# Signs of the second weight's slices by ScalarE, and another order of all engines, in a gated-linear-attention and hardswish kernel

## The chip, the cores and the metric

The kernel runs on one core of a Trainium2 chip. Times are device microseconds (us) of one execution. The kernel before took 536.4 us, the median of three runs (536.31 to 536.47). The core's engines work side by side, each through its own queue in order: TensorE (PE, with its weight loads as PEld), VectorE (DVE), ScalarE (ACT), GpSimd (POOL), and SyncE (SP), which here only issues DMAs. They wait for one another by semaphores.

## What is computed

Attention (4 batches, 8 heads, 768 tokens, 48 channels a head) is a linear recurrence with a decay for each channel; its output, as a matrix of 3072 tokens by 384, goes through a feed-forward block with 2048 hidden units. In the reference, cut to what matters:

```python
for t in range(S):
    state = alpha[:, :, t, :, None] * state + np.einsum('bhd,bhe->bhde', k[:, :, t], v[:, :, t])
    y[:, :, t] = np.einsum('bhd,bhde->bhe', q[:, :, t], state)
x = y.transpose(0, 2, 1, 3).reshape(B * S, H * D)
h = x @ w_in                                  # 384 x 2048
g = h * np.clip(h + 3.0, 0.0, 6.0) / 6.0
out = g @ w_out                               # 2048 x 384
```

q, k, v and alpha are float32. w_in and w_out arrive as float64[...], so the kernel receives them as pairs of 32-bit words and makes float32 out of them.

## The kernel before

**Tiles.** The sequence is cut into 24 chunks j of 128 tokens, six to a batch; two chunks form a group g of 256 tokens, so there are 12 groups.

**Attention of a chunk.** `la`, `lk`, `lq`, `lv` load alpha, k, q, v. For j below 6 TensorE turns them (`ta`, `tk`, `tq`, four transposes each) and ScalarE copies alpha (`ca`); later chunks are turned on VectorE. `r` and `p` are two scans on VectorE that give the decays; `k` and `q` scale by them. `kb` and `ck` bring k into token order (from chunk 8 on by way of DRAM: `kt`, `kw`, `kr`). `sc` and `m` give the masked scores, `qa` and `sv` are ScalarE's copies that place q and the state beside them, `u` and `sm` update the state, `st` (GpSimd) decays it, `ya` and `yb` form the output on TensorE, and `cy` (ScalarE) keeps it as x.

**Feed-forward.** Groups 0 and 1 use plain matmuls for the first weight: `f.g.i` gives 256 of the hidden units, `fa` and `fb` the same for one chunk of group 0 at a time, so that work can begin when only chunk 0 is there. Each fills one of four PSUM banks, from which `fr` (ScalarE, L494) and `fg` (VectorE, L498) form g. Group 0 uses plain matmuls for the second weight too (`b`). From group 2 on the first product runs over combined operands: 25 sums of weight blocks (`y`), 11 sums of x in each group (`xc`), 20 products `M` of which each is four matmuls, kept (`n`), added up (`o`), gated (`e`, `h`). From group 1 on the second product is seven products `P` with sums `s` of g and four sums `x` of the weight; `K` and `G` take the results out of PSUM, `O` stores them.

**The weights' way to float32.** There are 16 slices: 0 to 7 of w_in (256 columns each, so that slice i is what `f.g.i` needs) and 8 to 15 of w_out (two of the 16 row blocks each). `w.i` loads a slice of 768 KB into one of five raw buffers, two of which lie in the space of g of group 1 and serve only slices 3 and 4; the slices of w_out go through three. On it work:

- `d1` (ScalarE, L186): the low word is scaled and rounded, in place.
- `d2` (ScalarE, L196): the magnitude of the high word is written as float32 to the weight's place.
- `d3` (VectorE): for slices in `BY_HALVES` two operations, a clamp (L203) and a shift (L205). For the others three: a clamp (L207), a shift with mask (L208) and an operation with two tensors that puts the sign and top bits back (L210).
- `dx` (ScalarE, L191), for slices in `BY_HALVES` only: writes a float16 zero with the sign of the number into the upper half of the low word, so that the sign comes with the low word.
- `d4` (GpSimd, L217): adds low and high words, as integers.

A raw buffer can be loaded anew when `d4` has read it.

**The order.** There is no scheduler at run time: `run()` near L750 splits one long string, and every word calls its step. The words' order is each engine's order, and the queue of DMAs on SP as well. `z.m.n` are n matmuls on the identity into bank m, which compute nothing that is used.

Of the kernel before, what the change touches and what calls it, by code (L numbers as in the profile page):

```python
# [17 lines left out]
def kernel(  # L18
# [42 lines left out]
    G = 2  # L61
# [114 lines left out]
    BY_HALVES = {0, 1, 2, 4}  # L176
# [395 lines left out]
    for i in range(8):  # L572
        r, o = divmod(i, 3)
# [176 lines left out]
    with tc.manual_schedule():  # L750
        run("""z.0.5 z.0.3 z.0.1 z.0.8 qa.0.0 w.0 d2.0 d3.0 la.0 ta.0.0 ca.0 r.0 lk.0 tk.0.1 k.0
               z.0.2 p.0 la.1 ta.1.2 lq.0 tq.0.3 ca.1 r.1 lk.1 lv.0.0 sv.0.0 d1.0 kb.0.0 ck.0 z.0.2
               u.0.2.1 sm.0.0 sv.0.1 q.0 qa.0.1 tk.1.0 k.1 p.1 z.0.2 sc.0.2.3 m.0 la.2 ta.2.0 ca.2
               dx.0 w.2 d2.2 kb.1.0 ck.1 lq.1 r.2 sm.0.1 st.1 tq.1.2 q.1 d3.2 z.0.3 d1.2 dx.2 lv.1.1
               u.1.3.1 sv.1.0 sm.1.0 p.2 sm.1.1 sc.1.0.2 m.1 ya.0.3 yb.0 cy.0 lq.2 w.1 d1.1 tq.2.1
               q.2 d4.2 lk.2 tk.2.3 k.2 fa.2.0 d4.0 st.2 sc.2.0.2 d2.1 d3.1 m.2 dx.1 d4.1 qa.1.1
               lk.3 la.3 ta.3.1 ca.3 la.4 fa.0.1 sv.1.1 w.3 r.3 ta.4.3 ca.4 r.4 tk.3.1 k.3 kb.2.0
               qa.1.0 d2.3 ya.1.2 yb.1 cy.1 fa.1.2 lq.3 ck.2 d1.3 p.3 d3.3 lv.2.2 u.2.3.2 sm.2.0
               d4.3 fb.2 tq.3.1 q.3 fb.1 qa.2.0 sm.2.1 sv.2.0 st.3 fr.0.2.0 fg.0.2 lk.4 tk.4.0
               sv.2.1 w.5 d2.5 k.4 d3.5 d1.5 qa.3.0 d4.5 qa.2.1 sc.3.1.3 m.3 w.6 d2.6 d1.6 d3.6 d4.6  # L760
               lv.3.0 lq.4 w.7 kb.3.2 fb.0 f.0.3.3 kb.4.0 ya.2.1 ck.3 u.3.3.2 sm.3.0 fr.0.3.1 fg.0.3
               fr.0.1.0 fg.0.1 qa.3.1 sv.3.0 sm.3.1 p.4 d2.7 sv.3.1 d1.7 d3.7 d4.7 f.0.5.0 fr.0.5.1
               fr.0.0.0 fg.0.5 fg.0.0 tq.4.3 ck.4 la.5 ta.5.2 f.0.6.3 ca.5 w.4 d2.4 ya.3.0 yb.3 cy.3
               fr.0.6.1 yb.2 cy.2 w.9 d2.9 q.4 qa.4.1 d1.4 d1.9 dx.4 la.6 w.8 d3.4 r.5 lk.5 w.10
               d3.9 p.5 ca.6 fg.0.6 d4.9 w.12 lq.5 lv.4.1 d2.8 d3.8 f.0.7.2 d1.8 st.4 d4.8 d4.4 w.11
               fr.0.7.0 fg.0.7 f.1.7.0 fr.1.7.1 fg.1.7 sc.4.0.2 m.4 f.1.1.1 fr.1.1.0 fg.1.1 f.1.3.3
               fr.1.3.1 d2.10 d1.10 tk.5.3 f.1.0.2 d2.12 d3.10 d4.10 w.13 fg.1.3 fr.1.0.0 fg.1.0 k.5
               d3.12 lq.6 f.1.6.0 f.1.2.1 u.4.1.0 sm.4.0 d1.12 d4.12 sv.4.0 qa.4.0 ya.4.2 fr.1.6.1
               fg.1.6 w.15 tq.5.3 fa.4.3 sv.4.1 d2.11 kb.5.1 d2.13 fr.1.2.0 f.1.4.2 fr.1.4.1 d1.11
               sm.4.1 q.5 r.6 d3.11 d3.13 fg.1.4 d4.11 lv.5.0 lk.6 tq.6 p.6 d2.15 d3.15 fg.1.2 d1.13  # L770
               d4.13 sc.5.0.3 yb.4 f.1.5.0 fr.1.5.1 fg.1.5 tk.6 m.5 b.1.0.2 fb.4 b.1.1 d1.15 d4.15
               st.5 y.5 w.14 la.7 lk.7 cy.4 d2.14 qa.5.1 ck.5 b.0.0.1 fr.0.4.0 d3.14 k.6 q.6 ca.7
               fg.0.4 d1.14 d4.14 x.0 y.1 y.10 b.0.1 y.0 y.2 u.5.2 P.1.0.0 K.1.0 qa.5.0 sv.5.0
               qa.6.1 P.1.1.3 b.0.2 b.1.2 kb.6.0 ya.5.3 y.6 s.1.0.0 sm.5.0 sv.5.1 G.1.0.0 tk.7
               s.1.1.1 s.1.2.3 x.1 yb.5 cy.5 b.1.3 sc.6.1.2 lv.6.2 ck.6 u.6.3.0 s.1.3.2 x.2 P.1.2
               b.0.3 K.1.1 y.7 s.1.4 s.1.5 y.11 y.3 r.7 xc.2.1 x.3 y.4 y.8 xc.2.3 k.7 xc.2.0 xc.2.4
               y.9 y.12 y.16 y.13 y.15 P.1.3.3 K.1.2 P.1.4 bo.1 P.1.5 xc.2.5 G.1.1.1 P.1.6 y.14 y.17
               y.19 xc.2.6 sm.6.0 G.1.2.2 y.20 M.2.0.2 lv.12.1 la.8 O.1.1 O.1.0 ca.8 y.18 y.21 y.23
               so.1 G.1.3.3 n.2.0.8 bo.0 lq.7 lv.7.0 O.1.2 m.6 xc.2.2 xc.2.10 xc.2.7 tq.7 r.8 p.7
               xc.2.8 sv.6.1 M.2.15.3 M.2.1 kb.7.3 n.2.1.9 M.2.16 M.2.2 n.2.2.10 M.2.7.0 n.2.7.11  # L780
               sm.6.1 xc.2.9 q.7 p.8 M.2.3 M.2.4 n.2.4.12 M.2.8 o.2.0.0 M.2.5 n.2.5.13 qa.7.0 sv.6.0
               st.7 lk.8 O.1.3 lq.8 lk.9 la.9 la.10 tk.8 tq.8 lq.10 lq.9 ya.6.1 yb.6 M.2.9 z.1.3
               M.2.18.1 o.2.1.0 e.2.1.1 M.2.10 cy.6 ck.7 sc.7.0.2 u.7.1.3 n.2.10.14 M.2.11 qa.7.1
               ca.9 la.11 y.22 M.2.6.2 h.2.1 q.8 m.7 e.2.0.0 h.2.0 n.2.11.15 qa.6.0 n.2.18.10 qa.8.1
               M.2.12 M.2.19 n.2.12.12 M.2.13 sm.7.0 sv.7.1 r.9 k.8 o.2.3.0 sv.7.0 ya.7.0 y.24
               o.2.5.0 n.2.13.12 o.2.2.0 yb.7 cy.7 sc.8.1.2 xc.3.1 o.2.2.1 e.2.2.1 xc.3.3 o.2.3.1
               M.2.14 xc.3.4 xc.3.0 xc.3.5 o.2.4.0 xc.3.7 xc.3.6 o.2.6.0 P.2.0.1 M.3.0.2 M.2.17
               h.2.2 o.2.6.1 e.2.3.0 h.2.3 o.2.7.0 K.2.0 n.3.0.12 M.3.1 n.3.1.9 e.2.5.1 M.3.7.0
               n.3.7.13 xc.3.8 o.2.7.1 xc.3.2 kt.8 e.2.6.0 h.2.6 tk.9 M.3.2 n.3.2.10 e.2.4.0 P.2.1.3
               h.2.4 h.2.5 s.2.0.14 e.2.7.0 G.2.0.1 h.2.7 M.3.3 M.3.4 n.3.4.8 k.9 s.2.1.11 M.3.8  # L790
               o.3.0.0 ca.10 kt.9 P.2.3.3 s.2.2.15 s.2.3.14 lv.8.2 kw.8 kr.8 lk.10 sm.7.1 xc.3.9
               M.3.5 n.3.5.11 K.2.2 e.3.0.1 xc.3.10 M.3.9 o.3.1.0 P.2.2 K.2.1 u.8.0.3 M.3.18.2 s.2.5
               M.3.10 n.3.10.14 n.3.18.15 e.3.1.0 s.2.4 P.2.4 tq.9 h.3.0 st.8 sv.8.0 M.3.11 n.3.11.8
               tk.10 p.9 sm.8.0 q.9 r.10 k.10 qa.9.0 qa.9.1 m.8 sm.8.1 h.3.1 M.3.19 o.3.5.0 kt.10
               P.2.5 G.2.2.0 st.9 M.3.12 sc.9.0.1 qa.8.0 n.3.12.10 o.3.3.0 kw.9 lv.9.0 kr.9 sv.8.1
               u.9.2.3 sm.9.0 sv.9.1 sv.9.0 G.2.1.2 sm.9.1 st.10 M.3.15.2 M.3.16 M.3.6.3 M.3.13 m.9
               o.3.4.0 o.3.6.0 tq.10 n.3.13.10 o.3.2.0 e.3.4.1 ya.8.2 yb.8 ya.9.3 yb.9 cy.9 M.3.14
               M.3.17 cy.8 xc.4.1 P.2.6 e.3.5.0 G.2.3.3 o.3.2.1 xc.4.3 h.3.4 xc.4.4 o.3.6.1 xc.4.5
               xc.4.0 xc.4.6 e.3.2.1 M.4.0.0 n.4.0.10 P.3.0.1 xc.4.7 o.3.7.0 p.10 h.3.5 o.3.3.1
               xc.4.8 M.4.7.3 M.4.1 xc.4.2 h.3.2 o.3.7.1 lk.11 O.2.2 tk.11 e.3.6.0 e.3.3.1 h.3.3  # L800
               P.3.1.2 e.3.7.1 n.4.1.13 M.4.2 K.3.0 ca.11 q.10 h.3.6 r.11 k.11 h.3.7 n.4.7.15
               lv.10.2 lv.11.0 kw.10 sc.10.0.1 kr.10 G.3.0.0 u.10.3.2 sm.10.0 qa.10.1 n.4.2.14 M.4.3
               M.4.4 M.4.8 s.3.0.9 xc.4.9 s.3.2.12 s.3.1.11 P.3.3.2 n.4.4.8 M.4.5 o.4.0.0 e.4.0.0
               sv.10.1 sm.10.1 xc.4.10 kt.11 O.2.0 O.2.3 lq.11 m.10 s.3.3.9 s.3.5 M.4.9 o.4.1.0
               P.3.2 sv.10.0 st.11 n.4.5.11 K.3.2 la.13 M.4.18.0 p.11 tq.11 lk.12 tk.12 K.3.1 M.4.10
               n.4.10.9 q.11 qa.10.0 n.4.18.12 e.4.1.1 la.12 s.3.4 ca.12 h.4.0 r.12 P.3.5 G.3.2.1
               h.4.1 M.4.11 P.3.4 n.4.11.8 M.4.12 n.4.12.14 qa.11.0 M.4.19 p.12 G.3.1.3 lq.12 kw.11
               O.2.1 tq.12 kr.11 u.11.3 sc.11.0.2 sv.11.0 O.3.1 lk.13 P.3.6 qa.11.1 M.4.6.2 G.3.3.2
               k.12 o.4.3.0 m.11 sm.11.0 sv.11.1 kt.12 M.4.13 n.4.13.14 q.12 o.4.3.1 e.4.3.0 o.4.2.0
# [123 lines left out]
```

## Time and profile before

| | |
|---|---|
| Median of three runs | 536.4 us |
| The profiled execution | 536.33 us |
| Its span in the profile | 534.5 us |
| TensorE: first matmul, first that counts, end of the last | 1.46, 7.46, 530.7 us |
| f.0.3 (first whole `f`) starts | 40.08 us |
| First product `P` starts | 94.13 us |
| First product `M` starts | 125.70 us |
| Sign operation on ScalarE, L191 | 4 times, 1.93 us |
| L203, L205 on VectorE | 4 times each, mean 0.86 and 0.70 us |
| L207, L208, L210 on VectorE | 12 times each, mean 0.71, 0.60 and 0.96 us |
| L217 on GpSimd, slices by halves and others | 4 times, mean 1.91 us; 12 times, mean 1.60 us (least 1.46) |

The span begins with the first instruction and ends with the last store's landing; some 1.8 us of the execution lie around it. A share of busy time is the union of an engine's instructions over the span. Matmuls overlap, so that the time from one start to the next (the pitch) is less than the duration of one, and the same holds, by less, for VectorE and ScalarE.

### The profile page before, as it was taken

The numbers are of one execution on the slowest core, as the hardware profiler recorded it, in microseconds if no ns is written. First come the engines' busy times: TensorE is split into PE (matmuls) and PEld (weight loads), VectorE is DVE, ScalarE is ACT, GpSimd is POOL, SyncE is SP. The second block draws the span as 40 slices with busy tenths as digits, with TensorE's granted clock in tenths as the row PEclk, the third lists the DMA queues.
The fourth block names the chain that finished last, engine by engine and source line by source line (L and its number), as shares of the span: only waits on it lengthen the run. The fifth ranks groups of instructions, "written<-read, shape, count | busy, mean of one in ns | idle before, by whom it ended". The sixth has DMA issues, their size and how long they took to land.

```text
span 534.5 us, 15145 instructions
## 1 busy us (share of the span) xinstructions
PE 524.2 (98%) x6306; PEld 498.9 (93%) x6306; DVE 477.1 (89%) x849; ACT 257.6 (48%) x503; POOL 50.4 (9%) x71
## 2 busy tenths in 40 slices
PE   7799999999999999999999999999999999999997
PEld 7698886789999999999999999999999999999996
DVE  6999989999999899998999999999999898586381
ACT  3889864212653553543644434642633544553330
POOL 5333435100000000000010000000000000000000
PEclk9999999999999999999999999999999999999999
DMA  9998877006615155254354455055364042100001
GB/s 174 215 255 256 208 220 164 7 2 158 149 32 121 28 132 130 50 136 101 82 109 113 95 124 139 20 129 122 81 144 97 18 97 48 36 3 1 29 1 44
DMA packets 124100, 54.40 MB, mean 102 GB/s; under 512 B 83328, under 2 KB 116864, under 8 KB 124032
## 3 DMA queue, kind: packets, MB, share of 16 engines
q1 hardware_dynamic: 124032, 53.44, 43.0%
q8 instruction: 49, 0.80, 0.7%
q14 instruction: 19, 0.16, 0.1%
HBM read 44.50 MB, written 8.91 MB: 100 GB/s over the span
## 4 chain that ended last, share of the span: by engine, by line
PE 88%; DVE 6%; POOL 2%; ACT 1%; DMA 1%; issue 0%; SPq 0%; DVEq 0%; POOLq 0%
PE m_ps L703 34%; PE m_ps L600 34%; PE m_ps L478 6%; PE t_ps L455 4%; PE t_ps L346 2%; PE t_ps L429 2%; PE m_ps L489 2%; DMA v<-in_v_dram 1%; PE m_ps L516 1%; DVE rings L647 1%; PE t_ps L282 1%; DVE raw L537 1%; ACT raw L191 1%; DVE g_sb L647 1%; DVE w L537 1%; POOL v L96 1%
## 5 line engine op out<-in xcount | busy, mean ns | idle before, releaser
L606 ACT COPY g_sb<-m_ps 128x512 f32<-128x512 f32 x110 | 63.7, 584 | 124.1 <-PE m_ps L600 101.3
L703 PE MATMUL m_ps<-w,g_sb 128*128 128x192 f32 x704 | 121.7, 327 | 0.0
L703 PEld LDWEIGHTS m_ps<-w,g_sb 128*128 128x128 f32 x704 | 113.7, 190 | 0.4
L703 PE MATMUL m_ps<-rings,g_sb 128*128 128x192 f32 x528 | 91.5, 326 | 0.0
L703 PEld LDWEIGHTS m_ps<-rings,g_sb 128*128 128x128 f32 x528 | 85.4, 190 | 0.1
L600 PE MATMUL m_ps<-xc,w 128*128 128x128 f32 x640 | 82.7, 277 | 0.3 <-DVE w L541 0.3
L600 PEld LDWEIGHTS m_ps<-xc,w 128*128 128x128 f32 x640 | 77.5, 192 | 1.5 <-issue 0.5
L494 ACT ACTIVATE r<-g_sb,half 128x512 f32<-128x512 f32 x80 | 57.0, 722 | 31.5 <-DVE g_sb L541 12.4
L498 DVE SCALAR_TENSOR_TENSOR g_sb<-r,g_sb 128x512 f32<-128x512 f32 x80 | 53.7, 682 | 6.8 <-ACT r L494 5.4
L600 PE MATMUL m_ps<-xT,raw 128*128 128x128 f32 x400 | 52.5, 277 | 0.0
L600 PEld LDWEIGHTS m_ps<-xT,raw 128*128 128x128 f32 x400 | 48.6, 192 | 0.6
L409 POOL TENSOR_TENSOR st<-sm,R 128x192 f32<-128x192 f32 x20 | 12.9, 643 | 353.7 <-DVE sm L439 295.7
L647 DVE TENSOR_TENSOR g_sb<-g_sb 128x512 f32<-128x512 f32 (+1 forms) x55 | 42.1, 793 | 1.3 <-PE m_ps L703 1.1
L600 PE MATMUL m_ps<-xT,w 128*128 128x128 f32 x320 | 42.0, 276 | 0.0
L600 PEld LDWEIGHTS m_ps<-xT,w 128*128 128x128 f32 x320 | 39.3, 192 | 0.1
L366 ACT COPY A<-q 48x256 f32<-48x256 f32 x88 | 35.5, 404 | 5.0 <-DVE q L332 3.7
L356 DVE TENSOR_TENSOR A<-t_ps,mask 64x256 f32<-64x256 f32 x96 | 36.0, 413 | 0.4
L478 PE MATMUL m_ps<-xT,w 128*128 128x256 f32 x144 | 32.8, 382 | 0.0
L600 PE MATMUL m_ps<-xc,raw 128*128 128x128 f32 x240 | 31.8, 276 | 0.0
L478 PEld LDWEIGHTS m_ps<-xT,w 128*128 128x128 f32 x144 | 26.7, 190 | 3.6
L309 DVE TENSOR_TENSOR_SCAN R<-t,ones 128x516 f32<-128x516 f32 x24 | 29.6, 1233 | 0.5 <-ACT t L300 0.4
L600 PEld LDWEIGHTS m_ps<-xc,raw 128*128 128x128 f32 x240 | 29.6, 192 | 0.1
(104 smaller groups left out, 730.3 us busy)
## 6 DMA issues: line engine op xcount, KB each, us to landing
raw<-in_moe_w_out_dram SPq DMA_DIRECT2D x8, 768.0 KB, 5.3
raw<-in_moe_w_in_dram SPq DMA_DIRECT2D x6, 768.0 KB, 7.1
v<-in_v_dram SPq DMA_DIRECT2D x48, 96.0 KB, 3.0
out_dram<-oh SPq DMA_DIRECT2D x44, 96.0 KB, 1.7
far<-kq SPq DMA_DIRECT2D x64, 64.0 KB, 2.2
kb<-far SPq DMA_DIRECT2D x64, 64.0 KB, 2.1
aq<-in_alpha_dram SPq DMA_DIRECT2D x36, 96.0 KB, 2.4
qq<-in_q_dram SPq DMA_DIRECT2D x36, 96.0 KB, 2.5
```

Source lines behind the costliest of these rows:

```text
L309: nc.vector.tensor_tensor_scan(out=reverse(R, n - 1, n), data0=reverse(ax, n, n), data1=reverse(ones, n, n), initial=0.0, op0=ALU.mult, op ...
L356: nc.vector.tensor_tensor(out=to[:, a], in0=sc[a][half], in1=mask[half, half].unsqueeze(1).to_broadcast([HB, NP, HB]), op=ALU.mult)
L366: nc.scalar.copy(out=to[:, a], in_=Q_t[j][64 * a : 64 * a + D, :, half])
L409: nc.gpsimd.tensor_tensor(out=st, in0=sm, in1=R_t[j][:, :, 0:1].to_broadcast([C, NP, D]), op=ALU.mult)
L455: nc.tensor.matmul(y_of(j, (i + 1) // 2, p)[:, HB * b : HB * b + HB], vb[:, p, e : e + 32], A_t[j][:, b, 2 * p + a], start=(b == 0 and i = ...
L478: nc.tensor.matmul(h[:, f], w1[:, kk, o : o + C], xT_t[g][:, kk], start=(kk == 0), stop=(kk == KT - 1))
L494: nc.scalar.activation(out=to, in_=h, func=AF.Relu, bias=half, scale=1.0 / 6.0)
L498: nc.vector.scalar_tensor_tensor(out=to, in0=r, scalar=1.0, in1=h, op0=ALU.min, op1=ALU.mult)
L600: nc.tensor.matmul(acc[g][i][:, f * C : (f + 1) * C], spots[w][:, f * C : (f + 1) * C], x_of(g, x), start=(first and f == 0), stop=last, s ...
L606: nc.scalar.copy(out=slots[z], in_=acc[g][i])
L647: nc.vector.tensor_tensor(out=out, in0=in0, in1=in1, op=ALU.subtract)
L703: nc.tensor.matmul(to[g], a, rhs[:, f], start=(first and f == 0), stop=(last and f == HF - 1), skip_group_check=True)
```

## The change

It has two parts. The first adds slices 8 to 15, all of w_out, to `BY_HALVES`: their `d2` gets another scale, their `d3` has two operations instead of three, each of them needs a `dx`, and `d4` reads the high word from the weight's place instead of the raw buffer. The second replaces the whole string of words: the same steps for everything else, with other banks and other places for kept tiles, in another order. The number of `z` matmuls is 29 in both. The eight `dx` are the only words added.

```diff
-    BY_HALVES = {0, 1, 2, 4}
+    BY_HALVES = {0, 1, 2, 4, *range(8, 16)}
...
-        run("""z.0.5 z.0.3 z.0.1 z.0.8 qa.0.0 w.0 d2.0 d3.0 la.0 ta.0.0 ca.0 r.0 lk.0 tk.0.1 k.0
-               z.0.2 p.0 la.1 ta.1.2 lq.0 tq.0.3 ca.1 r.1 lk.1 lv.0.0 sv.0.0 d1.0 kb.0.0 ck.0 z.0.2
-               u.0.2.1 sm.0.0 sv.0.1 q.0 qa.0.1 tk.1.0 k.1 p.1 z.0.2 sc.0.2.3 m.0 la.2 ta.2.0 ca.2
-               dx.0 w.2 d2.2 kb.1.0 ck.1 lq.1 r.2 sm.0.1 st.1 tq.1.2 q.1 d3.2 z.0.3 d1.2 dx.2 lv.1.1
...
-               s.11.1.14 s.11.3.10 P.11.3.2 K.11.0 s.11.2.11 o.11.2.1 o.11.3.1 P.11.2 K.11.2
-               e.11.2.0 h.11.2 s.11.4 e.11.3.1 h.11.3 P.11.1.0 s.11.5 G.11.0.1 O.11.0 O.10.3 K.11.1
-               P.11.4 G.11.1.2 P.11.5 G.11.2.1 O.11.2 P.11.6 G.11.3.0 O.11.3 O.9.2 O.11.1""")
+        run("""z.0.1 z.0.2 z.0.2 z.0.3 z.0.8 qa.0.0 w.0 d1.0 d2.0 d3.0 la.0 ta.0.0 ca.0 lk.0 z.0.3
+               tk.0.1 r.0 k.0 p.0 dx.0 d4.0 w.2 d2.2 d3.2 lq.0 lv.0.0 sv.0.0 z.0.5 z.0.2 kb.0.2
+               tq.0.3 q.0 ck.0 u.0.0.1 d1.2 dx.2 d4.2 sc.0.2.3 qa.0.1 sm.0.0 sm.0.1 m.0 la.1 ta.1.0
+               ca.1 r.1 p.1 st.1 ya.0.1 sv.0.1 yb.0 w.1 d2.1 d3.1 lq.1 tq.1.0 q.1 cy.0 fa.0.0 la.2
+               ta.2.2 d1.1 dx.1 lk.1 tk.1.3 k.1 fa.2.1 ca.2 r.2 kb.1.1 sc.1.0.2 m.1 qa.1.1 qa.1.0
+               lv.1.1 ck.1 u.1.3.1 sm.1.0 sv.1.0 d4.1 fa.1.2 w.3 d2.3 d3.3 sm.1.1 p.2 sv.1.1 ya.1.0
+               yb.1 lk.2 tk.2.2 k.2 st.2 d1.3 d4.3 lq.2 tq.2.3 q.2 cy.1 fb.0 fb.2 w.5 d2.5 fr.0.0.0
+               fg.0.0 d1.5 d3.5 d4.5 sc.2.0.1 m.2 qa.2.1 w.6 d2.6 qa.2.0 kb.2.2 fb.1 ck.2 w.7 d2.7
+               d3.7 f.0.3.3 fr.0.1.1 fg.0.1 d1.7 d4.7 la.3 ta.3.3 lv.2.2 sv.2.0 u.2.2.0 sm.2.0
+               f.0.5.0 fr.0.3.0 ya.2.1 d1.6 fg.0.3 d3.6 d4.6 sv.2.1 yb.2 f.0.7.2 fr.0.2.1 ca.3 la.4
+               w.4 lk.3 tk.3.2 d1.4 d2.4 dx.4 w.8 d2.8 d1.8 cy.2 dx.8 f.0.6.3 fg.0.2 sm.2.1 d3.4 r.3
+               k.3 d3.8 kb.3.3 lq.3 d4.4 tq.3.0 fa.4.1 lq.4 lv.3.0 ck.3 u.3.2.1 st.3 sv.3.0 p.3 q.3
+               qa.3.0 fr.0.6.0 sm.3.0 sv.3.1 sm.3.1 sc.3.0.3 m.3 fb.4 lk.4 tk.4.2 ta.4.1 w.9 fg.0.6
+               fr.0.5.1 fg.0.5 ya.3.0 qa.3.1 ca.4 yb.3 cy.3 d4.8 r.4 st.4 k.4 p.4 d1.9 fr.0.7.0
+               fg.0.7 fr.0.4.1 fg.0.4 la.5 lv.5.1 w.11 d2.9 d1.11 tq.4.3 q.4 ta.5.1 ca.5 f.1.3.3
+               kb.4.0 ck.4 fr.1.3.0 dx.9 f.1.7.0 fr.1.7.1 la.6 ca.6 d3.9 lv.4.2 u.4.2.1 r.5 sc.4.0.3
+               m.4 sm.4.0 d2.11 dx.11 sv.4.0 d4.9 d3.11 qa.4.0 w.10 d2.10 d1.10 dx.10 d4.11 fg.1.3
+               sm.4.1 st.5 lq.7 lk.6 tk.6 fg.1.7 d3.10 r.6 f.1.1.2 fr.1.1.0 f.1.0.1 lk.5 tk.5.0
+               fg.1.1 k.6 p.5 lq.6 w.12 d1.12 fr.1.0.1 k.5 fg.1.0 d2.12 d3.12 f.1.6.3 fr.1.6.0 dx.12
+               b.1.0.0 lq.5 tq.5.3 f.1.2.2 la.7 ca.7 fg.1.6 w.14 d1.14 lk.7 sv.4.1 fr.1.2.1 d2.14
+               lk.8 kb.5.2 qa.4.1 ck.5 dx.14 f.1.5.1 fr.1.5.0 d4.10 w.13 d2.13 d1.13 d4.12 w.15
+               d1.15 la.8 b.0.0.3 b.1.1 b.0.1 q.5 p.6 sc.5.0.1 d3.14 tq.6 fg.1.2 q.6 r.7 d3.13
+               s.1.1.1 d2.15 d3.15 dx.13 dx.15 fg.1.5 d4.14 y.0 y.1 u.5.3 ca.8 m.5 d4.13 lv.6.0 la.9
+               sv.6.0 f.1.4.2 sv.5.0 fr.1.4.1 fg.1.4 tk.7 d4.15 y.3 y.9 sm.5.0 b.1.2 b.1.3 P.1.0.1
+               P.1.1.2 kb.6.2 y.6 s.1.0.0 y.5 x.0 x.1 sv.5.1 ya.4.0 yb.4 qa.5.1 bo.1 qa.5.0 ya.5.1
...
+               h.11.2 o.11.3.1 e.11.3.0 h.11.3 P.11.1.2 G.11.0.0 O.11.0 K.11.1 P.11.4 K.11.2 s.11.5
+               G.11.1.0 O.11.1 P.11.5 G.11.2.0 O.8.3 O.10.3 P.11.6 G.11.3.1 O.11.2 O.9.1 O.11.3""")
```

## The prediction

> **What bounds the kernel now.** I read the busy shares first, then the chain of work that ended last, then the table of 10 us windows, and then the time lines of each engine up to 130 us and of the last 5 us. The page's shares and the windows:
>
> ```profile
> PE 524.2 (98%) x6306; PEld 498.9 (93%) x6306; DVE 477.1 (89%) x849; ACT 257.6 (48%) x503; POOL 50.4 (9%) x71
> ```
> ```profile
> 10.00:20.00 10.00, 6.87 (x104) 5.67 (x104) 9.31 (x17) 7.37 (x12) 0.09 (x1) 1.00 1.29 228
> 20.00:30.00 10.00, 8.84 (x208) 7.90 (x207) 9.84 (x19) 9.70 (x14) 6.81 (x5) 1.00 0.97 217
> ...
> 80.00:90.00 10.00, 10.00 (x44) 6.99 (x43) 9.83 (x14) 5.96 (x11) 5.97 (x10) 1.00 0.70 165
> ...
> 120.00:130.00 10.00, 9.71 (x71) 9.55 (x70) 9.87 (x23) 2.57 (x6) 0.00 (x0) 1.00 0.56 143
> ```
>
> The columns after the stretch and its length are PE, PEld, DVE, ACT, POOL, clock, DMA share and GB/s. TensorE is full in every window from 40 us on, but for 0.29 us at 127.9; VectorE is above 97% from 20 to 130 us in all windows but one (70 to 80: 85%). The chain's pieces say which of the two decides there:
>
> ```profile
> 108.89 2.34 DVE g_sb L647 x3
> 111.23 0.60 DVE raw L537
> ...
> 127.10 0.70 DVE w L541
> 127.80 0.14 issue
> 127.93 1.13 PE m_ps L600 x8
> ```
>
> From 92.1 to 127.8 the chain is VectorE almost without a break, and from 127.93 to 530.74 it is TensorE. So the first part is a balance of two full engines, which VectorE loses by 0.3 us, and the rest is pure matmul.
>
> To see where TensorE loses time I added up its work in the written order by pitch (starts, one after another, in the time line: a `P` product 2.60, an `M` product 0.90, a whole `f` 2.63, a half one 1.34, a `b` 2.60, four transposes 0.44, `sc` and `u` 0.62, `ya` or `yb` 0.59). Ahead of f.0.3 stand 26.7 us and it started at 40.08: 13.4 us lost. Ahead of M.2.0 stand 111.7, start 125.70: 14.0. Ahead of P.11.0 497.8, start 512.53: 14.7. **The loss is made before 40 us**; afterwards there is nothing to win but the tail. VectorE's sum before P.1.0 is 86.0 and P.1.0 began at 94.13, so VectorE had lost 8.1 us, all at the very start.
>
> **What the Trainium skill says.** "VectorE: DVE Perf Modes", section The perf-mode tier table: fp32 tensor_scalar runs at twice the rate of operations with two tensors. The trace agrees: L207 and L208 took 0.55 and 0.56 us for 768 columns, L210, which has two tensors, 0.96. "GPSIMD Engine Reference", section Key points: GpSimd shares its SBUF interfaces with VectorE and contends with two-port modes and two-input operations. The trace agrees: an L207 at 82.38, under a GpSimd add, took 1.77 instead of 0.56. "ScalarE: Activation LUTs", section What ACT_TABLE_LOAD costs: an operation with immediate scale takes 186 ns and 0.833 ns per element, 0.83 us for 768. The trace has 0.93 for the plain kinds (pitch 0.83), but 1.93 for the sign operation, which the page would not give; the measured value is used.
>
> **The change, part by part.**
>
> *VectorE.* For slices 8 to 15 the three operations L207, L208, L210 become two, L203 and L205:
>
> ```profile
> 52.17 0.68 DVE L203 TENSOR_SCALAR w<-w 128x768 f32<-128x768 f32 x1
> 52.89 0.69 DVE L205 TENSOR_SCALAR w<-w 128x768 uint32<-128x768 uint32 x1
> ...
> 69.04 0.55 DVE L207 TENSOR_SCALAR w<-w 128x768 f32<-128x768 f32 x1
> 69.62 0.56 DVE L208 TENSOR_SCALAR w<-w 128x768 uint32<-128x768 uint32 x1
> 70.22 0.96 DVE L210 SCALAR_TENSOR_TENSOR raw<-raw,w 128x768 uint32<-128x768 uint32 x1
> ```
>
> From start to start the pair took 1.33 and the triple 2.03 to 2.3 (mean 2.15). Eight times 0.82 is 6.6 us off VectorE, in its full stage.
>
> *ScalarE.* Eight sign operations, pitch 1.68 (16.72 to 18.39, 56.45 to 58.12): plus 13.4 us. Its sum from f.0.3 to f.1.4, the last `f` in the new order, is 51.3 us, while TensorE's over the same words is 53.7. In the old order the like stretch (f.0.3 to f.1.5) has 31.1 of 38.9. The cover has shrunk from 20% to 4%; the rival below is made of this.
>
> *GpSimd.* The low-half add takes 1.9 us instead of 1.5 (L217 by form: means of 1.93 and 1.86, against rows of 1.47 where nothing disturbs it): 8 times 0.4, 3.2 us, of a queue with 50 busy us in the whole span. It now waits for the sign operation too; behind it on GpSimd stand `st` and the next adds, behind those the state copies and `ya`. Its indirect cost is contention with VectorE: between 0 and the whole 3.2 us; I take 0.5.
>
> *The order.* The number of idle matmuls is 29 in both. I walked the new first 40 us by hand. Loads: the queue landed w.0 at 5.6, lq.0 (four small loads on) at 10.5 and lv.0 at 13.07 (two more), so a small load of 192 KB costs 1.2 us; slices two and three of the page (215 and 255 GB/s) then leave 2.6 us for a weight slice. In the new queue that gives w.2 10.6, lq.0 11.8, lv.0 13.0, la.1 14.2, w.1 16.8, lq.1 18.0, lk.1 20.4, w.3 24.2, lq.2 26.6, w.7 34.4, la.3 35.6, lv.2 36.8.
> VectorE, ends: d3.0 8.9, p.0 11.85, d3.2 13.2, q.0 13.8, m.0 15.95, p.1 18.3, d3.1 19.65, q.1 20.25, k.1 21.6 (0.75 waiting for lk.1), r.2 22.85, m.1 24.4, d3.3 27.4 (0.55 waiting for w.3), p.2 28.8, q.2 30.0, fg.0.0 30.6, d3.5 32.8, m.2 34.3, d3.7 37.5 (1.0 waiting for w.7), fg.0.1 38.1. Its work up to there is 28.0: lost 10.1, 2.0 more than before.
> ScalarE, next free: dx.0 10.3, dx.2 14.4, ca.1 15.8, d2.1 18.1 (waits for w.1, cy.0 behind it), cy.0 18.4, dx.1 20.9, ca.2 21.5, ck.1 23.6, d2.3 25.2, cy.1 27.3.
> TensorE: cy.1 is out at 27.3, then fb.0, fb.2, sc.2, kb.2, fb.1 bring f.0.3 to 32.8, with 22.8 us of work ahead of it: lost 10.0. Then ta.3 and u.2 wait 0.7 for their loads: 10.7, against 13.4. **TensorE gains 2.7 us.**
>
> That gain is worth what VectorE can follow. Behind the weights, the place where VectorE was nearest to TensorE in the old order is P.2.3, which needs s.2.1: TensorE's sum ahead of it is 146.3, VectorE's up to it 146.4. In the new order the nearest is P.2.2 with s.2.3: 149.6 and 145.2. The distance grows from -0.1 to 4.3, by 4.4 us (6.6 from the weights, the rest is spent by work placed earlier). Since there was nothing to spare at 127.9, VectorE allows 4.4 less its 2.0 more of early loss, less 0.5 of contention: 1.9. The smaller counts: **1.9 us**. Bounds: 0 (all of it eaten by loads that land late), and 3.7 (no early loss of 2.0 and no contention let VectorE allow 4.4, and no wait of 0.7 for ta.3 and u.2 lets TensorE gain 3.4, plus 0.3 from the wait at 127.9).
>
> *The tail.* In the kernel before, SP still issues three stores after the last output copy:
>
> ```profile
> 530.77 0.32 ACT oh L716
> ```
> ```profile
> 531.11 0.81 SPq L724 DMA_DIRECT2D out_dram<-oh  x2
> ```
> ```profile
> 531.97 0.43 SPq L724 DMA_DIRECT2D out_dram<-oh  x1
> ```
>
> Two of the three (O.9.2, O.11.1) had been ready for long. In the new order O.11.2 and O.9.1 stand ahead of O.11.3 and can go before 530.7, so only the first issue is left: 531.97 less 531.11 is **0.86 us**. From the start of the last issue to the span's end it stays 2.5. If SP is still behind, 0.4.
>
> *The M and P stage*, 130 to 530: the same products, TensorE full. VectorE's distance grows further from there in both orders (old 9.8, new 16.7 at the nearest places from sum 280 on); I cost the reordering at 0, from -0.3 to +2.
>
> Sum: 1.9 + 0.86 = 2.8. The profiled execution took 536.33 with a span of 534.5; 536.33 - 2.8 = 533.5. It stands 0.07 below the median, which I leave.
>
> **Rivals.**
> *ScalarE becomes the bound of the weight stage (slower).* It serves in order: `fr` empties the banks of `f`, and a sign operation, or a d1 or d2 whose slice has not landed, stands ahead of it. It decides once ScalarE waits over 3 us in all between 33 and 88 us (TensorE's 53.7 less 51.3, and some 0.6 for the last `fr`). For it: before, ScalarE waited 3.6 and 3.2 us for two single slices (L196). Against it: `fr` of f.1.4 has b.1.2, b.1.3 and P.1.0, 7.8 us, behind it on TensorE before its result is needed. With 8 us of waits TensorE is 5 late: 533.5 + 5 = 538.5. Chance 0.22.
> *Only the tail is won.* Three weight slices in the first seven loads hold back lv.0, la.1 and lk.1; if each small load costs 1.4 and each slice 3.1, w.7 lands 5 us later and the 1.9 is gone: 536.33 - 0.86 = 535.5, no change in the terms below. For it: the first 13 us ran at 174 GB/s only. Chance 0.16.
> *More is won than walked*, 3.7 and 0.86: 531.8, and up to 1 more if waits in the walk are all covered: 530.8. It is in the first case's upper end, with 0.04 beyond.
>
> **Numbers.** A measurement of this kernel can tell 0.2%, 1.07 us, from no change. Main case 0.58 (531.7 to 535.2), more 0.04: faster 0.62. Tail only: same 0.16. ScalarE: slower 0.22. The range goes from 530.8 to 538.5, with about half of the ScalarE case and little of the other end left out.
>
> **What would show it.** Right: P.1.0 and M.2.0 begin about 2 us earlier against their sums (M.2.0's 110.5 of work starting near 122.5), f.0.3 near 33, the last copy on ScalarE followed by a single store. VectorE without waits from 38 to 128. Wrong: TensorE gaps between 35 and 95 that end on ScalarE's L494 or L186 or on GpSimd's L217 (first rival), or f.0.3 after 35.5 with waits on loads (second).

## The result, and the profile after

The kernel after took 536.56 us (median of 20 runs, 535.12 to 539.16), the kernel before 536.57 in the same session (20 runs, 536.21 to 537.98): a ratio of 1.000, 95% interval 0.9993 to 1.0008. **No change, where 533.5 was predicted.** The profiled execution of after took 537.53 (span 535.8), 1.0 above its median, and that of before 536.33, 0.2 below; so the two traces differ by 1.2 us where the medians don't. Its executions also scatter over 4.0 us, twice those of before.

The page's shares after:

```profile
PE 523.3 (98%) x6306; PEld 499.6 (93%) x6306; DVE 476.1 (89%) x841; ACT 270.3 (50%) x511; POOL 55.7 (10%) x71
```

ScalarE has the 12.7 us more that eight sign operations were to cost (13.4). VectorE has eight instructions less, and yet only 1.0 us less, where 6.6 were predicted: **5.6 us of the saving don't show in VectorE's busy time.** Most of that are instructions that took longer, as the ledger below shows. The windows, in the columns of the prediction:

```profile
10.00:20.00 10.00, 7.15 (x152) 5.98 (x152) 9.53 (x15) 8.44 (x13) 4.73 (x4) 0.84 1.28 199
20.00:30.00 10.00, 9.54 (x189) 8.76 (x188) 9.79 (x17) 9.07 (x16) 1.85 (x1) 0.99 1.05 281
...
80.00:90.00 10.00, 10.00 (x37) 6.66 (x36) 9.27 (x10) 8.13 (x12) 3.68 (x2) 1.00 0.95 244
...
120.00:130.00 10.00, 8.64 (x112) 8.10 (x110) 9.93 (x20) 1.49 (x4) 0.00 (x0) 1.00 0.38 92
```

Between 80 and 90 us VectorE is 93% busy with 10 instructions, before 98% with 14. The chain of work that ended last, after:

```profile
81.85 8.53 DMA raw<-in_moe_w_out_dram
...
93.33 0.67 DVE g_sb L498
...
107.77 0.60 DVE raw L539
...
128.90 0.10 DVE q L332
...
129.74 0.61 DVE w L541
130.35 0.14 issue
130.49 2.52 PE m_ps L600 x20
```

From 93.33 VectorE leads the chain up to 130.35, 2.5 us longer than before. From 56.48 to there it runs mainly over three loads of the second weight (8.56, 6.85 and 8.53 us), other loads between them and one of GpSimd's adds, where before it was TensorE's up to 89.5; whether these loads decide is tested below. TensorE's waits up to 132 us (what waits, for what; total, times, longest) are now mostly for VectorE too:

```profile
PE t_ps L346 <- DVE q L332: 3.1, 2, 2.3
PE m_ps L600 <- DVE w L541: 1.6, 1, 1.6
PE t_ps L282 <- DMA rings<-in_q_dram: 1.5, 1, 1.5
```

By TensorE's sums, counted as in the prediction: 12.0 us are lost before f.0.3 (start 34.84; predicted 10.0, before 13.4), but 16.3 before M.2.0 (start 126.77; before 14.0). TensorE's early gain was lost again by 127 us. The tail is as predicted, one store behind the last copy:

```profile
532.97 0.32 ACT L716 COPY oh<-m_ps 128x192 f32<-128x192 f32 x1 [9.86 <-PE m_ps L703]
```

From the start of this copy to the span's end it took 2.79 us (532.97 to 535.76), before 3.75 (530.77 to 534.52): 0.96 won.

**Where VectorE's time went.** For each VectorE instruction up to the one at which M.2.0 begins, take its duration less the tenth percentile of the same line and shape in the same trace, and put it under "beside GpSimd" if a GpSimd instruction overlapped it. This ledger is good to about 1 us in its sums.

| us up to M.2.0 | idle | longer, beside GpSimd | longer, else |
|---|---|---|---|
| before | 7.5 | 4.4 | 0.5 |
| after | 10.2 | 9.1 | 1.1 |

In the kernel before, two VectorE instructions are over 0.5 us too long beside a GpSimd add (2.5 us together), in the kernel after seven (8.0 us). One of the seven, from VectorE's and GpSimd's time line:

```profile
87.09 1.86 POOL L217 TENSOR_TENSOR w<-w,raw 128x768 int32<-128x768 int32 x1 [5.27 <-ACT raw L191]
87.13 2.90 DVE L309 TENSOR_TENSOR_SCAN R<-t,ones 128x516 f32<-128x516 f32 x1
```

and the same pair 14 us before, the other way round:

```profile
73.02 1.23 DVE L309 TENSOR_TENSOR_SCAN R<-t,ones 128x516 f32<-128x516 f32 x1
73.34 2.56 POOL L217 TENSOR_TENSOR w<-w,raw 128x768 int32<-128x768 int32 x1 [1.84 <-DVE w L205]
```

The scan that began 0.04 us after the add ended 1.08 us after the add's end: it took almost its whole 1.22 us then. The scan that began first took its 1.23, and the add waited instead (2.56, not 1.86). So one holds the other up for whole instructions, and the first comer wins. This is what the Trainium skill says, "SBUF — State Buffer", section Who interferes with whom: VectorE shares a pair of SBUF ports with GpSimd, held for a whole instruction by whoever starts first; it is needed by VectorE instructions in a two-port mode or with two SBUF inputs, the latter only against a GpSimd instruction that reads SBUF. A scan has two inputs in SBUF. The prediction had cited only that there is contention, and priced it as if bandwidth were shared.

### The profile page after: what moved, and what is told of

Read it like the earlier page. It is cut to its first block, busy times and chain, and to the rows that moved or that the text cites. A ratio compares the mean times of both kernels' runs of the same rounds, so it can differ in the third digit from the quotient of the medians.

```text
span 535.8 us, 15118 instructions
## 1 busy us (share of the span) xinstructions
PE 523.3 (98%) x6306; PEld 499.6 (93%) x6306; DVE 476.1 (89%) x841; ACT 270.3 (50%) x511; POOL 55.7 (10%) x71
## 4 chain that ended last, share of the span: by engine, by line
PE 82%; DVE 9%; DMA 6%; issue 1%; SPq 1%; ACT 1%; POOL 0%; DVEq 0%; POOLq 0%; ACTq 0%
PE m_ps L600 34%; PE m_ps L703 34%; DMA raw<-in_moe_w_out_dram 4%; PE t_ps L455 4%; PE t_ps L346 2%; PE t_ps L429 2%; PE m_ps L478 2%; PE m_ps L489 2%; PE m_ps L532 1%; DVE raw L537 1%; DVE P L320 1%; DVE rings L647 1%; DMA kq<-in_k_dram 1%; PE t_ps L282 1%; DVE A L356 1%
## 5 line engine op out<-in xcount | busy, mean ns | idle before, releaser
L494 ACT ACTIVATE r<-g_sb,half 128x512 f32<-128x512 f32 x80 | 56.7, 722 | 48.4 <-DVE g_sb L541 24.9
L409 POOL TENSOR_TENSOR st<-sm,R 128x192 f32<-128x192 f32 x20 | 14.7, 736 | 344.9 <-DVE sm L439 287.4
L600 PEld LDWEIGHTS m_ps<-xT,w 128*128 128x128 f32 x320 | 39.2, 192 | 0.4
L309 DVE TENSOR_TENSOR_SCAN R<-t,ones 128x516 f32<-128x516 f32 x24 | 31.7, 1319 | 0.6 <-ACT t L300 0.5
L320 DVE TENSOR_TENSOR_SCAN P<-t 128x516 f32<-128x516 f32 x24 | 31.2, 1299 | 0.1
L537 DVE TENSOR_TENSOR g_sb<-g_sb 128x512 f32<-128x512 f32 x40 | 26.8, 683 | 4.7 <-ACT g_sb L606 4.5
```

What stands on the lines that cost most here:

```text
L309: nc.vector.tensor_tensor_scan(out=reverse(R, n - 1, n), data0=reverse(ax, n, n), data1=reverse(ones, n, n), initial=0.0, op0=ALU.mult, op ...
L320: nc.vector.tensor_tensor_scan(out=P_t[j], data0=aX[j % 2][:, 0:n], data1=ini[j % 2], initial=0.0, op0=ALU.mult, op1=ALU.add)
L494: nc.scalar.activation(out=to, in_=h, func=AF.Relu, bias=half, scale=1.0 / 6.0)
L537: eng.tensor_tensor(out=out, in0=in0, in1=in1, op=ALU.add if s1 > 0 else ALU.subtract)
L600: nc.tensor.matmul(acc[g][i][:, f * C : (f + 1) * C], spots[w][:, f * C : (f + 1) * C], x_of(g, x), start=(first and f == 0), stop=last, s ...
```

## The experiments

**Two theories.** Theory 1, contention: VectorE, which sets the start of M, lost what it had won by standing still beside GpSimd's adds. An instruction stands still when it has begun and doesn't advance; the trace shows it as a longer instruction, not as a wait. Theory 2: the new round of the weights' loads and buffers lets the weights land late, and TensorE waits for that.

### The parts alone

`order_only` has the new order without the new signs, `signs_only` the old order with them, `tail_only` the kernel before with two stores moved.

```diff
# order_only: after, with
-    BY_HALVES = {0, 1, 2, 4, *range(8, 16)}      and without dx.8 to dx.15
+    BY_HALVES = {0, 1, 2, 4}
# signs_only: before, with
+    BY_HALVES = {0, 1, 2, 4, *range(8, 16)}      and each dx.i ahead of d4.i
# tail_only: before, with
-    P.11.6 G.11.3.0 O.11.3 O.9.2 O.11.1
+    O.9.2 O.11.1 P.11.6 G.11.3.0 O.11.3
```

> The new order without the eight sign operations; slices 8 to 15 keep three VectorE operations, as before. Theory 1 (VectorE's 6.6 us went to contention with GpSimd's longer adds): VectorE gets the 6.6 us back as work but loses some 2 us of contention, M.2.0 some 3 to 4 us later than in the changed kernel, 539 to 541 us. Theory 2 (the weights' round of load, sign, add and buffer, behind it the queue of SP, makes TensorE wait between 50 and 96 us): each round is 1.7 us shorter on ScalarE and 0.4 on GpSimd, the waits of 1.5 and 0.7 us at 75 and 96 vanish, 536 to 538 us.

> The order of before, with the eight sign operations put in directly ahead of each slice's add. Theory 1: VectorE's gain of 6.6 us is worth 0.3 us here at most, since the order keeps TensorE full from 40 us on anyway; the longer adds cost little where the adds lie under operations with PSUM operands; 536.0 to 537.0. Theory 2: each slice's buffer comes free 2 us later, loads slip, TensorE waits for the last slices near 90 us: 537.5 to 540.

> The kernel before, with O.9.2 and O.11.1 put ahead of P.11.6, so that the last copy is followed by one store. Both theories: 0.86 us less, 535.5 to 535.8. If the last store's landing isn't what ends the run: no change.

| | median us (runs) | ratio to before, 95% interval |
|---|---|---|
| order_only | 544.23 (4) | 1.0136 (1.0120 to 1.0151) |
| signs_only | 539.72 (5) | 1.0057 (1.0044 to 1.0070) |
| tail_only | 535.46 (13) | 0.9979 (0.9971 to 0.9987) |

**The new order alone costs 7.7 us** (7.4 against the kernel before as it ran beside it), more than either theory had said, and the signs win 7.7 in it (6.7 in the profiled executions, 544.27 against 537.53). That this is near the 6.6 of the prediction is luck. The prediction took the pair's 1.33 us from a slice of w_in; for a slice of w_out after's time line has

```profile
66.02 0.55 DVE L203 TENSOR_SCALAR w<-w 128x768 f32<-128x768 f32 x1
66.61 0.56 DVE L205 TENSOR_SCALAR w<-w 128x768 uint32<-128x768 uint32 x1
67.08 0.68 DVE L498 SCALAR_TENSOR_TENSOR g_sb<-r,m_ps 128x512 f32<-128x512 f32 x1
```

that is 1.06 from the pair's start to the next instruction's, and 1.04 to 1.10 for all of slices 8 to 15 but one that stood still. The triple took 2.03 to 2.09 in order_only, where undisturbed. So some 8.0 us of work went (an estimate, eight times 1.0), and VectorE stood still 1.9 longer beside GpSimd than in order_only (9.1, not 7.2).

Most of the order's cost is in the ledger: 18.6 us up to M.2.0 (idle 10.9, beside GpSimd 7.2, else 0.5) against 12.4, so 6.2; the prediction's 2.2 of work placed earlier, less 0.96 of tail, make it 7.4, where the profiled executions differ by 7.9. Of the 6.2, 3.4 are idle time and 2.8 are beside GpSimd.

The signs alone, in the old order, cost 3.2 us, a time in theory 2's range. What VectorE waited for there fits the prediction's rival, in which ScalarE becomes the bound. VectorE's waits from 20 to 132 us in signs_only:

```profile
DVE g_sb L498 <- ACT r L494: 5.2, 5, 2.0
DVE w L203 <- ACT w L196: 2.9, 2, 2.2
```

It waited 3.9 us more for two of GpSimd's adds (L217). It sat idle for 17.7 us up to M.2.0, while ScalarE was 93% busy from 50 to 90 us; beside GpSimd it lost 4.2, no more than before. Neither the order nor the signs win without the other; only the tail does, with 1.1.

### The adds made small

`low_cut` and `cut_first` cover only a part of the columns in the adds named below, so that the weights lack most of their low parts. An add made small also ends sooner, and its raw buffer comes free sooner; the runs after these take that apart.

```diff
# low_cut: after, in add_low            # cut_first: the same for i == 0
+        if i >= 8:
+            dst, high, lo = dst[:, :, 0:16], high[:, :, 0:16], lo[:, :, 0:16]
```

> The changed kernel, whose adds for slices 8 to 15 cover 32 of the 768 columns, so that 96 per cent of the second weight is left without its low part; all waits stay. Theory 1: the stalls of VectorE under these adds (0.8, 1.7 and 1.7 us between 74 and 95) are gone, M.2.0 starts 3 to 4 us earlier, 532.5 to 534. Theory 2: the round is 1.8 us shorter, the waits at 75 and 96 us shrink by that, but VectorE is not earlier than by 1 us: 535 to 536.

> The changed kernel, with the add of slice 0 alone cut to 48 of its 768 columns, so that most of this slice lacks its low part. Theory 1: the scan L320 that took 2.89 us under this add takes 1.2, f.0.3 starts 1.2 to 1.7 us earlier than 34.84, the end is 1 to 1.7 us earlier, 535 to 535.5, since VectorE is the bound at M.2.1. Theory 2: f.0.3 is earlier, the end is not: 536.2 to 537.

`low_cut` took **533.47** (4 runs; ratio 0.9942, 0.9923 to 0.9961), 3.1 less than after: the time predicted for the change. VectorE's busy time, in low_cut's page, fell by 4.5 us though it has the same work:

```profile
PE 523.6 (98%) x6306; PEld 500.0 (94%) x6306; DVE 471.6 (88%) x841; ACT 270.7 (51%) x511; POOL 42.9 (8%) x71
```

`cut_first`, with one add small, took 535.37 (20 runs; 0.9979, 0.9971 to 0.9987), also as theory 1 had it; its profiled execution, 538.3, was the slowest of its 20, so that its trace doesn't show the median's gain. The add of slice 0 stands beside the first scan of p:

```profile
10.65 1.85 POOL L217 TENSOR_TENSOR w<-w,raw 128x768 int32<-128x768 int32 x1 [3.65 <-ACT raw L191]
10.70 2.89 DVE L320 TENSOR_TENSOR_SCAN P<-t 128x516 f32<-128x516 f32 x1
...
15.55 0.69 PE L346 MATMUL t_ps<-q,k 48*64 48x64 f32 x32 [2.28 <-DVE q L332]
```

That is after's time line. The scan came 1.67 us late, q.0 behind it, and TensorE waited 2.28 us for q.0.

### The loads

```diff
# queue: after, with lq.5 ahead of w.12
# short_load: after, in load_weight for slices 8 to 15
-                out=to, in_=moe_w_out[o : o + m * C, :]
+                out=to[:, :, 0:192], in_=moe_w_out[o : o + m * C, 0:192]
```

> The changed kernel with lq.5 put ahead of w.12 in SP's queue. Its wait of 1.47 us on TensorE at 75 us goes in any case. Theory 1: VectorE is late at M.2.1 all the same, 536 to 536.7. Theory 2: 1 to 1.5 us less, 535 to 535.6.

> The changed kernel whose loads of slices 8 to 15 bring only the first quarter of each row; the rest of the raw buffer holds what was there, so that most of the second weight is wrong. All waits stay, the loads land 3 us earlier or more. Theory 1: 535.5 to 536.5, only VectorE's waits of some 2.5 us between 60 and 100 us shrink. Theory 2: 533 to 534.5.

They took 537.12 (12 runs; 1.0006, 0.9994 to 1.0019) and 537.02 (12 runs; 1.0008, 0.9999 to 1.0016). Both are about 0.5 us above what theory 1 had expected, and 2 to 3 above theory 2. Neither a quarter of the bytes nor another place in the queue helps, though in short_load no load of the weights stands in the chain any more (it runs mainly over ScalarE up to 67 us and over VectorE from 70 us), and in queue TensorE's wait of 1.5 for q is gone. **Theory 2 alone falls.** That both bounds lie close together, so that shorter rounds would pay once VectorE stands still less, isn't excluded by these runs.

### The adds cut in pieces

The whole add is done, in several instructions.

```diff
# split_add: after, all slices; split_some: slice 0 by 256, 8 to 15 by 192, others whole;
# split_two: as split_some, but 8 to 15 by 384
-        nc.gpsimd.tensor_tensor(out=dst..., in0=high..., in1=lo..., op=ALU.add)
+        for m in range(dst.shape[1]):
+            for n in range(0, dst.shape[2], cut):
+                at = slice(n, n + cut)
+                nc.gpsimd.tensor_tensor(out=dst[:, m, at]..., in0=high[:, m, at]..., ...)
```

> The changed kernel with every low-half add on GpSimd cut into pieces of at most 256 and 192 columns (three for a slice of the first weight, four for one of the second), nothing left out. Theory 1 (VectorE operations with two SBUF inputs or in a two-port mode stand still until a GpSimd add that has begun is over, and the adds of 1.85 us cost VectorE 9.1 us up to 132 us, 4.4 before): the stall per meeting is at most a piece, the sum falls to 4 to 6 us, 532.5 to 534.5. Theory 2 (the round of the weights' loads decides): the round isn't shorter, 536 to 537.

> The kernel after, with only the adds that ran into VectorE's work cut in pieces: slices 8 to 15 in four pieces of 192 columns, slice 0 in its three rows of 256; the others whole. In the run with all adds cut, slice 4 was late by the cutting and TensorE waited 1.43 us for it. Contention theory (VectorE stands still while a whole GpSimd add runs): VectorE's stretch under adds falls from 9.1 to 3.5 to 4.5 us, no wait for slice 4, 534.0 to 535.5. If what the pieces cost on GpSimd is what limits them: like the run with all adds cut, 535.8, or later.

> As the run before this one, but slices 8 to 15 in only two pieces of 384 columns. Contention theory: if VectorE waits at most for the end of the piece that runs, it waits about half as long as for a whole add; stretch 5 to 7 us, 535 to 536.3. If what counts is the sum of the time in which adds run, whatever their pieces: 536.6, as after.

(In split_add the w_in slices came out in six pieces, 192 and 64 columns in each of three rows, not three.)

| | median us (runs) | ratio to before, 95% interval | beside GpSimd |
|---|---|---|---|
| split_add | 535.78 (21) | 0.9985 (0.9978 to 0.9991) | 3.9 |
| split_some | 536.27 (14) | 0.9996 (0.9981 to 1.0010) | 5.5 |
| split_two | 535.80 (21) | 0.9986 (0.9978 to 0.9994) | 7.2 |

**Inconclusive in size.** VectorE's loss beside GpSimd fell in all three traces, but the medians fell by 0.3 to 0.8 only, less than theory 1 expected but for split_two; split_some is not distinct from before. The profiled executions of split_some and split_two took 534.37 and 535.05, below their medians, so those traces show a good case. So of low_cut's 3.1 us it is not shown how much came from less standstill and how much from the rounds, which it shortened too; pieces with short loads, or the kernel before with small adds, were not run. In split_add the cutting had a price of its own, a later slice 4 (TensorE's time line):

```profile
49.39 1.16 PE L493 MATMUL m_ps<-xT,w 128*128 128x128 f32 x8 [1.43 <-POOL w L220]
```

### The adds doubled, and a control

Fewer or shorter adds also leave GpSimd free and release buffers earlier. `double_add` does each add of slices 8 to 15 a second time into dead space, `busy_memset` two memsets of that space, about as long, in its place.

```diff
# double_add: after, behind the add, for i >= 8
+            nc.gpsimd.tensor_tensor(out=hi.bitcast(I32), in0=dst.bitcast(I32),
+                                    in1=lo.bitcast(I32), op=ALU.add)
# busy_memset: in its place
+            for _ in range(2):
+                nc.gpsimd.memset(hi.bitcast(FP), 0.0)
```

> The kernel after, and GpSimd does a second add of the same size behind each add of slices 8 to 15 (two inputs in SBUF, result into the spent high word of the raw buffer, which nothing reads). The weight itself is ready as early as before; the raw buffer comes free some 1.9 us later and GpSimd has 15 us more to do. Contention theory: VectorE's stretch under adds grows from 9.1 us by as much again as slices 8 to 15 cause, 4 to 6 us, and the time to 539 to 542. If what counts is only when buffers come free and when GpSimd is done (occupation theory): it and the next run come out alike.

> The control to the run before it: behind each add of slices 8 to 15 GpSimd does two memsets of the spent high word instead of a second add, so that it is occupied, and the buffer held, for about as long, but reads nothing from SBUF. Contention theory: stretch clearly less than with the second add, and 536.5 to 538.5. Occupation theory: the same time as with the second add.

`double_add` took **547.62** (5 runs; ratio 1.0209, 1.0191 to 1.0227), `busy_memset` **539.59** (5 runs; 1.0054, 1.0042 to 1.0067): 8.0 us apart. The same scan of chunk 6, in double_add beside the second add (L220; line numbers are three higher here):

```profile
87.95 1.85 POOL L220 TENSOR_TENSOR raw<-w,raw 128x768 int32<-128x768 int32 x1
88.08 2.81 DVE L323 TENSOR_TENSOR_SCAN P<-t 128x516 f32<-128x516 f32 x1
```

and in busy_memset beside the memsets (L221):

```profile
85.20 1.68 POOL L221 MEMSET raw<- 128x768 f32 x2
85.46 1.23 DVE L323 TENSOR_TENSOR_SCAN P<-t 128x516 f32<-128x516 f32 x1
```

By the ledger VectorE lost 16.9 us beside GpSimd in double_add and 9.0 in busy_memset, against 9.1 in after: the second adds cost 7.9, the memsets nothing in the sum, and 7.9 is close to the difference of the two times. The scan was held up by the GpSimd instruction **that reads SBUF** and not by the one that only writes, as the skill's page says of VectorE instructions with two SBUF inputs. The clamp and the shift, each with one SBUF input, were held up by memsets too, also in busy_memset:

```profile
66.64 1.97 POOL L221 MEMSET raw<- 128x768 f32 x2
66.92 0.95 DVE L203 TENSOR_SCALAR w<-w 128x768 f32<-128x768 f32 x1
67.90 1.13 DVE L205 TENSOR_SCALAR w<-w 128x768 uint32<-128x768 uint32 x1
```

instead of 0.55 and 0.56. That fits the page's other case, the two-port modes, which contend whether GpSimd reads or not; the trace doesn't show the mode. Occupation costs something else: busy_memset is 3.0 us later than after, 1.1 above what theory 1 had expected of it and far below double_add. VectorE was idle 2.7 us longer (12.9, not 10.2): a constant memset of kq (L257) stood behind more work in GpSimd's queue, and VectorE waited 4.0 us for it (2.4 in after), and 1.1 for the last of the new memsets themselves. double_add waits for kq as well (4.3 us) and came out 5.6 later than theory 1's expectation.

### The new order with small adds

`order_low` is order_only with low_cut's edit.

> The new order without the eight sign operations (544.2), with the adds of slices 8 to 15 covering only 32 of their 768 columns, so that the output is not the reference's. Contention theory: that order too has 7.2 us of stretch under adds, of which these eight adds cause 3 to 4; so 540.3 to 541.5. If the cut adds helped the kernel after by having the weights ready earlier, and not by contention: 543.5 to 544.5, because here they wait for VectorE's third operation in any case.

540.92 (5 runs; ratio 1.0075, 1.0062 to 1.0088), as the contention theory had it: 3.3 less than order_only, and the ledger beside GpSimd fell from 7.2 to 5.2. Small adds win about the same with and without the signs on ScalarE, and signs_only, with the signs in the old order, lost no more beside GpSimd than before: **it is the order that put the adds in VectorE's way**, not the wait for the sign. In that order the signs then added 1.9.

### TensorE's clock early on

```diff
# warm: after, with
+    z.0.8 z.0.8 ahead of sc.0.2.3
```

> The kernel after, with 16 more idle matmuls ahead of the first scores, where TensorE waited 2.28 us and then ran at a granted clock of 0.84 for some microseconds (64 small matmuls took 2.01 us, not 1.10). If that loss of clock counts, TensorE wins up to 1.4 us before the first f; but VectorE is the engine that sets the start of M, so the contention theory expects 536.0 to 536.8, no difference. If TensorE's early loss is what takes the gain: 535.0 to 535.6.

538.83 (7 runs; ratio 1.0036, 1.0021 to 1.0051), outside both expectations, by a mistake of mine: the 16 matmuls took 3.84 us, not the 1.8 assumed, and pushed the scores 1.6 us back (17.13, after 15.55). The clock stayed at 1.00 as meant, but f.0.3 began 2.1 us later. So the loss of clock isn't priced by this run; what it shows is that 1.6 us of delay at 15 us come out as 2.3 at the end. There is no slack.

### The old order with pieces, and a better version

`tail_split` is tail_only with split_some's edit. `early_memset3` is after with the constant memsets of L257 done at the load of v of chunk 1; `early_two3` is that and split_two's edit.

```diff
# early_memset3: after, in load_akq
-        if j < FIRST + NQ:
-            for o in (BLK, 3 * BLK):
-                nc.gpsimd.memset(to[o : o + BLK, :, V - 1, D - BLK : BLK], 1.0)
# in load_v
+        if j == 1:
+            for to in quads.values():
+                for o in (BLK, 3 * BLK):
+                    nc.gpsimd.memset(to[o : o + BLK, :, V - 1, D - BLK : BLK], 1.0)
```

> The kernel before with the two ready stores moved ahead (535.46) and with the adds of slices 8 to 15 in four pieces of 192 columns, slice 0 in three. In the old order VectorE lost 4.4 us under adds, 2.6 of them between 80 and 100 us, and VectorE sets the start of M there. Contention theory: stretch about 2.5 us, so 533.5 to 534.8. If the adds' pieces end later than whole ones and TensorE then waits for the weights: 535.5 or later.

> The kernel after, with GpSimd's constant memsets of the turning buffers (L257) done all at once with the load of v of chunk 1, not with the first loads into each buffer, where they stand in GpSimd's queue behind the adds: VectorE waited 2.37 us for one at 70.41. Contention theory, with VectorE as the engine that sets the start of M: 534.2 to 535.5, the stretch under adds unchanged at about 9. If that wait is covered (TensorE being the bound there): 536.2 to 536.8.

> As the run before it, and the adds of slices 8 to 15 in two pieces of 384 columns, slice 0 in three (535.80 alone). Contention theory: both gains add up, 533.4 to 534.8, ahead of both kernels. If the pieces' gain was chance: as the run before it.

`tail_split`: 535.16 (14 runs; 0.9976, 0.9968 to 0.9984), not distinct from tail_only and above the 533.5 to 534.8 that theory 1 had expected. VectorE lost 1.4 us less beside GpSimd (3.1, not 4.5), but in the old order TensorE is as full as VectorE, and P.1.0 began at 94.90, in tail_only at 94.83. `early_memset3`: 536.37 (14 runs; 1.0000, 0.9992 to 1.0008), no gain, where theory 1 had expected 1.1 to 2.4. The wait for kq is gone, but the next in line took its place: VectorE's waits from 60 to 132 us,

```profile
DVE w L203 <- ACT w L196: 1.5, 1, 1.5
DVE g_sb L499 <- ACT r L495: 0.5, 1, 0.5
```

`early_two3`: **534.48** (6 runs; 0.9963, 0.9949 to 0.9976), ahead of both kernels by 2.1, and of split_two by 1.3. Why the early memsets win with pieces and not without is not settled; the traces show a like idle time (8.9 and 9.7) and a like loss beside GpSimd (7.3 and 7.4).

## Why the prediction was wrong

- **VectorE's 6.6 us**: under-sized. The pair was read off a slice of w_in (1.33); on the slices that changed it took 1.06, so some 8.0 us of work went. With the order held fixed the profiled executions differ by 6.7 only because more standstill took the rest.
- **ScalarE's 13.4 and the rival made of it**: 12.7 in busy time. No wait of TensorE in after ends on L494 or L186, and VectorE's waits for ScalarE between 60 and 132 us sum to 1.0. One wait of TensorE, 0.7 us at 96 us, ends on L217. The rival (538.5) didn't happen here; in the old order it did.
- **Early loss of VectorE, 2.0 more**: 2.7 more idle, a little under-sized, and not where it was put: up to 40 us after is only 0.2 above before (5.3 and 5.1). The largest single wait after 40 us, 2.4, is at 70 us, for the memset of kq behind the adds in GpSimd's queue.
- **TensorE's 2.7**: it lost 1.4 less before f.0.3, as the scan beside the first add delayed q.0.
- **GpSimd's contention, 0.5, with 3.2 as its bound: this is the step that failed.** It measured 4.7 (9.1 less 4.4). The bound was wrong in kind, though the prediction's own example, an L207 of 1.77 instead of 0.56, had stood still for 1.2. It took the part by which the adds grew longer, 8 times 0.4, as all that could collide. But a collision costs up to the whole add (1.67 us for a scan beside an add of 1.86), and whether it happens is set by what the order puts beside the add. In the order before, most adds lay beside VectorE instructions with an operand in PSUM, which ran at their usual time, as this one from before's time line:

```profile
67.24 1.28 DVE L498 SCALAR_TENSOR_TENSOR g_sb<-r,m_ps 128x512 f32<-128x512 f32 x2
67.46 1.47 POOL L217 TENSOR_TENSOR w<-raw 128x768 int32<-128x768 int32 x1 [2.14 <-ACT r L494]
```

  In the new order more lie beside scans, multiplications and the weights' clamps, whose inputs are in SBUF. I had costed the contention of the edit and not that of the order. By the ledger 2.8 of the 4.7 came with the order alone and 1.9 with the signs in it.
- **The allowance of 1.9**: 4.4 of distance less 2.7 less 4.7 less 0.6 of other lengthening is -3.6, not +1.9. TensorE's further loss at M.2.0 in the two profiled traces is 2.3. With 8.0 in place of 6.6 the distance is 5.8 and the sum -2.2; the ledger's error of 1 us allows no closer test.
- **The tail's 0.86**: 0.96 by the traces; alone it won 1.1.
- **M and P stage, 0**: right. From M.2.0's start to the last matmul's end it took 405.0 before and 406.2 after, and M.2.0 stands 1.2 us of work earlier in the new order.

So the medians' sum is a tail of 1.1 won and a weight stage of about 1.1 lost. low_cut, which has fewer collisions (4.3 us by the ledger), took 533.47, the predicted time. That is in part luck: its rounds are shorter too, and the prediction had VectorE's saving too small and TensorE's early gain too large.

## What to carry to other kernels

Before an order is changed, list for every long GpSimd instruction what VectorE does beside it; put such instructions beside VectorE work that ran at its usual time here (with a PSUM operand, or transposes), and price a collision at up to the whole length of the first comer, not at a share. Take a duration from the very tiles that change. Compare an engine's busy time with its instruction count: work was taken away here and the busy time stayed, which shows stalls inside instructions that no list of waits contains. Where two engines are full together, a gain in the one is worth only what the other can follow, so look for the next wait before counting it.

## What the runs showed of the hardware

- A VectorE instruction in its way stands still for the rest of a GpSimd add: scans of 1.22 us took up to 2.90, a clamp L203 of 0.55 up to 2.20 (in double_add), a multiplication from SBUF of 0.66 took 1.49. Adds beside instructions with a PSUM operand cost VectorE nothing, nor did an add beside a transpose, which kept its 1.13 (at 79.75 in after). Beside memsets of GpSimd scans kept their 1.22, while a clamp took 0.95 and a shift 1.13.
- The order of start decides, and a lead of 0.04 us was enough: a scan was late by 1.68 us in one case and the add by 0.70 in the other. Whether this is why the new order's executions scatter by 4 us was not tested.
- After TensorE had waited 2.28 us, its granted clock was 0.84 in the window from 10 to 20 us, where it was 1.00 in the kernel before, and 64 small matmuls took 2.01 us; with idle matmuls in the wait (warm) it was 1.00, and they took 0.67 and 0.81 in two parts.
